# Top-32 attention and a Sinkhorn mixture of experts on one core: the weight tile becomes the work buffer of top-32

## The chip, the core and the metric

The kernel runs on one core of one Trainium2 chip. The metric is the device time of one execution in microseconds. The engines named below are PE (TensorE, matmuls), DVE (VectorE), ACT (ScalarE), POOL (GpSimd) and SP (SyncE, which issues the DMAs here). Each engine takes its own instructions strictly in the order of the program and waits at semaphores for the others.

## What is computed

Two parts follow each other. The first is attention over 4 batches, 8 heads, 576 rows and head size 64, in which each row keeps only its 32 largest scores. The second is a mixture of 8 experts whose gate is balanced by 8 rounds of Sinkhorn normalisation over all 2304 rows.

```
scores = scale * np.matmul(q, k.transpose(0, 1, 3, 2))
kth = np.partition(scores, -top_k, axis=-1)[..., -top_k:-top_k + 1]
scores = np.where(scores >= kth, scores, -1000000000.0)
attn = np.exp(scores - max); attn = attn / (sum + 1e-09)
x = attn @ v
logits = x @ w_gate; P = np.exp(logits - logits.max())
for _ in range(8):
    P /= P.sum(1, keepdims=True) + 1e-09
    P /= P.sum(0, keepdims=True) + 1e-09
    P *= N / E
for e in range(E):
    out += P[:, e:e + 1] * (np.maximum(x @ w1[e], 0.0) @ w2[e])
```

## The kernel before

**Attention.** The work comes in 7 stages (one batch and one or two blocks of 256 query rows each), 80 top-32 jobs in all. A job is a pair of two units of 128 rows (64 jobs; the other 16 have one unit). For a unit PE forms a 128 x 576 tile of scores in PSUM (tile `sp`, L121 and L122), ACT copies it to a score buffer `s` (L130, 3 buffers). `topk` then runs on DVE: four times it takes the 8 largest (MAX8, L140), and between them three times it strikes those 8 out (MATCH_REPLACE8, L143). The first strike reads `s` and writes a work buffer `w` (2 buffers, one for each unit of a pair); the later ones work in `w`. Then ACT makes the weights from `s` and the threshold, in the tile `Et` that holds both units of a pair (L146, L147; 2 buffers), they are normalised (L150 to L156; the reciprocal L151 is on DVE), and PE transposes them (L239, L299) for the product with `v`.

**Experts.** Each visit of an expert loads weights (`wr`, 3 buffers), and splits them into a high part on ACT (`wh`, L80) and a low part on POOL (`wl`, L86), 6 buffers of each. PE multiplies them (L451, L564). ACT and DVE take the hidden values out of PSUM (L519, L520). Visits need only the x of their blocks, so they fill PE while attention goes on. Visits 20 to 23 handle one block of 256 rows alone.

**After attention.** `sinkhorn` runs 8 rounds on DVE; each has one tiny matmul against a tile of ones (L424). Then the attention pools are closed. The last part of the kernel computes the remaining row blocks by a Strassen-like scheme (`hidden_pair`, L675, then L734). Its right factors are built once by `right_factors`: sums `tf` on POOL (L627), high parts on ACT (`B11h`, `T1h`, ..., L80) and low parts on POOL (`B11l`, `T1l`, ..., L86). They live in a pool `x2` that is opened on the same side of the memory as the closed attention pool `ap_`. The left factors are sums on POOL (L661) and a split as above.

**What sets the order.** A scheduler orders the instructions of each engine by priority and by its own estimate of times. Attention has a higher priority than the visits. The tile of ones is allocated in the pool `const`, outside the attention pools:

```
    ones = const.tile([128, 128], F32, name="ones")
    nc.vector.memset(ones, 1.0)

    def sinkhorn():
```

Below, "the work of PE" between two places is the count of its matmuls there.

Of the kernel before, what the change touches and what calls it, by code (L numbers as in the profile page):

```python
# [7 lines left out]
F32 = mybir.dt.float32  # L8
# [4 lines left out]
NB, NH, S, D = 4, 8, 576, 64  # L13
# [28 lines left out]

PARKED = 4
ALONE, LATER = range(0, 4), range(4, 8)
WR, WB, XR, NS, RAW, YB = 3, 6, 3, 3, 3, 4


@with_exitstack
def kernel(
# [11 lines left out]
    nc = tc.nc  # L61
# [3 lines left out]
    const = ctx.enter_context(tc.tile_pool(name="const", bufs=1))  # L65
# [10 lines left out]
    ap_ = actx.enter_context(tc.tile_pool(name="ap", bufs=2, side="right"))  # L76
# [38 lines left out]
    def scores(groups):  # L115
        sp = pss.tile([128, 2, 512], F32, name="sp")
        for dst, terms in groups:
            o = sp[:, dst[0], dst[1]:dst[2]]
            n = len(terms)
            for i, (qc, (kh, kl), cs) in enumerate(terms):  # L120
                nc.tensor.matmul(o, qc, kh[:, cs], start=(i == 0), stop=False)  # L121
                nc.tensor.matmul(o, qc, kl[:, cs], start=False, stop=(i == n - 1))  # L122
        return sp

    def copy_scores(sp):
        s = ap_.tile([128, S], F32, name="s", bufs=NS)
        if sp.shape[-1] == S:
            nc.scalar.activation(s, sp, AF.Copy, scale=0.125)
        else:
            nc.scalar.activation(s.rearrange("p (a b) -> p a b", a=2), sp, AF.Copy, scale=0.125)  # L130
        return s

    def topk(units):
        n = len(units)
        ws = [ap_.tile([128, S], F32, name="w", bufs=2) for _ in units]
        m8 = ap_.tile([128, 2, 4, 8], F32, name="m8", bufs=3)
        eb = ap_.tile([128, 2], F32, name="eb", bufs=3)
        for r in range(4):
            for u in range(n):
                nc.vector.max(m8[:, u, r, :], ws[u] if r else units[u][0])  # L140
            if r < 3:
                for u in range(n):
                    nc.vector.match_replace(ws[u], m8[:, u, r, :], ws[u] if r else units[u][0], LOWEST)  # L143
        nc.gpsimd.tensor_tensor(eb[:, 0:n], m8[:, 0:n, 3, 7], m8[:, 0:n, 0, 0], op=OP.subtract)
        for u, (s, Em, rsum) in enumerate(units):
            nc.scalar.activation(Em, s, AF.Prelu, bias=m8[:, u, 3, 7:8], scale=-1.0, alpha=KEPT)  # L146
            nc.scalar.activation(Em, Em, AF.Exp, bias=eb[:, u:u + 1], scale=-1.0 / KEPT, accum_out=rsum)  # L147

    def normalise(Et, st, n, on_pool=False):
        nc.gpsimd.tensor_scalar(st[:, 0, 0:n], st[:, 0, 0:n], 1e-9, 1.0, op0=OP.add, op1=OP.mult)  # L150
        nc.vector.reciprocal(st[:, 1, 0:n], st[:, 0, 0:n])  # L151
        for i in range(n):
            if on_pool:
                nc.gpsimd.tensor_scalar(Et[:, i, :], Et[:, i, :], st[:, 1, i:i + 1], 1.0, op0=OP.mult, op1=OP.mult)
            else:
                nc.scalar.activation(Et[:, i, :], Et[:, i, :], AF.Copy, scale=st[:, 1, i:i + 1])  # L156
# [62 lines left out]

    def weight_tiles(qs, ks, put, on_pool=False):  # L220
        for t in range(2):
            Et = ap_.tile([128, 2, S], F32, name="Et", bufs=2)
            st = ap_.tile([128, 2, 2], F32, name="st", bufs=3)
            units = []
            for i in range(2):
                o = i * 256 + t * 128
                qc = qs[:, o:o + 128]
                sp = scores([((a, 0, 288), [(qc, ks[i], slice(a * 288, a * 288 + 288))]) for a in range(2)])
                units.append((copy_scores(sp[:, :, 0:288]), Et[:, i, :], st[:, 0, i:i + 1]))
            topk(units)  # L230
            normalise(Et, st, 2, on_pool)
            cs = slice(t * 128, (t + 1) * 128)
            Ef = Et.rearrange("p a b -> p (a b)")
            for g in range(3):
                ps = pst.tile([128, 4, 128], F32, name="pt")
                for r in range(3):
                    j = g * 3 + r
                    o = j * 128 if j < 4 else (j * 128 + 128 if j < 8 else 512)
                    nc.tensor.transpose(ps[:, r, :], Ef[:, o:o + 128], idt)  # L239
                put(slice(g * 3, g * 3 + 3), cs, ps[:, 0:3, :])  # L240
# [43 lines left out]


    def rest_weights(qm, ks, put):
        Et = ap_.tile([128, 2, S], F32, name="Et", bufs=2)
        st = ap_.tile([128, 2, 2], F32, name="st", bufs=3)
        qa, qb = qm[:, 0:128], qm[:, 128:256]
        sp = scores([  # L290
            ((0, 0, 256), [(qa, ks[0], slice(0, 256)), (qb, ks[1], slice(64, 320))]),
            ((0, 256, 512), [(qa, ks[0], slice(256, 512)), (qb, ks[1], slice(320, 576))]),
            ((1, 0, 64), [(qa, ks[0], slice(512, 576)), (qb, ks[1], slice(0, 64))]),
        ])
        topk([(copy_scores(sp.rearrange("p a b -> p (a b)")[:, 0:S]), Et[:, 0, :], st[:, 0, 0:1])])
        normalise(Et, st, 1)
        ps = pst.tile([128, 4, 128], F32, name="pt")
        for j in range(4):
            nc.tensor.transpose(ps[:, j, :], Et[:, 0, j * 128:(j + 1) * 128], idt)  # L299
        for i in range(2):  # L300
            put(slice(0, 128), slice(4 * i, 4 * i + 4), ps[:, :, i * 64:(i + 1) * 64])
        ps = pst.tile([128, 4, 128], F32, name="pt")
        nc.tensor.transpose(ps[0:64, 0, :], Et[:, 0, 512:576], idt)
        nc.tensor.transpose(ps[:, 1, :], Et[:, 0, 448:576], idt)
        for i, r in enumerate((va, vb)):
            put(r, 8, ps[r, i, r])
# [87 lines left out]
                hi_act(seat.xh[:, kk, cs], x[:, kk, :])  # L394
                lo_dve(seat.xl[:, kk, cs], x[:, kk, :], seat.xh[:, kk, cs])

    ones = const.tile([128, 128], F32, name="ones")
    nc.vector.memset(ones, 1.0)

    def sinkhorn():  # L400
        lgf = lg.rearrange("p t e -> p (t e)")
        mx = const.tile([128, 1], F32, name="mx")
        nc.vector.reduce_max(mx, lgf, axis=mybir.AxisListType.X)
        tp = pst.tile([128, 512], F32, name="pt")
        nc.tensor.transpose(tp[:, 0:128], mx.to_broadcast([128, 128]), idt)
        nmx = const.tile([128, 1], F32, name="nmx")
        nc.vector.reduce_max(nmx, tp[:, 0:128], axis=mybir.AxisListType.X)
        nc.vector.tensor_scalar(nmx, nmx, -1.0, None, op0=OP.mult)

        bank = pss.tile([128, 2, 512], F32, name="sp")  # L410
        Q = bank[:, 0, 0:NT * E].rearrange("p (t e) -> p t e", t=NT)
        rp, cp = bank[:, 0, 256:256 + NT], bank[:, 0, 320:320 + E]
        nc.scalar.activation(bank[:, 0, 0:NT * E], lgf, AF.Exp, bias=nmx)
        rs = const.tile([128, NT], F32, name="rs")
        cs = const.tile([128, E], F32, name="cs")
        cr = const.tile([128, E], F32, name="cr")
        for i in range(8):
            nc.vector.reduce_sum(rp, Q, axis=mybir.AxisListType.X)
            nc.vector.tensor_scalar(rp, rp, 1e-9, None, op0=OP.add)
            nc.vector.reciprocal(rs, rp)  # L420
            nc.vector.tensor_tensor(Q, Q, rs[:, :, None].to_broadcast([128, NT, E]), op=OP.mult)
            nc.vector.reduce_sum(cs, Q.rearrange("p t e -> p e t"), axis=mybir.AxisListType.X)
            ct = pst.tile([128, 512], F32, name="pt")
            nc.tensor.matmul(ct[:, 0:E], ones, cs, start=True, stop=True)  # L424
            nc.vector.tensor_scalar(cp, ct[:, 0:E], 1e-9, float(E) / N, op0=OP.add, op1=OP.mult)
            nc.vector.reciprocal(cr, cp)
            nc.vector.tensor_tensor(P if i == 7 else Q, Q, cr[:, None, :].to_broadcast([128, NT, E]), op=OP.mult)
# [412 lines left out]
```

## Time and profile before

| | us |
|---|---|
| median of 3 runs | 1922.92 (1922.9 to 1923.92) |
| the profiled execution, its own time | 1925.95 |
| its span, first to last instruction | 1924.2 |
| PE busy | 1878.1 (98%) |
| DVE busy | 1301.4 (68%) |
| ACT busy | 1108.7 (58%) |
| POOL busy | 1030.8 (54%) |

A busy PE is not PE at its peak, since matmuls overlap in the records; so time is counted here by the distance from one matmul to the next and by the stretches in which PE stands idle. A row of the timeline has the start in us, the busy time of the group in us, the engine, the line, the instruction and its tiles, and in brackets the idle time before it and what ended it.

### The profile page before, as it was taken

What the parts mean: (1) busy time and instruction counts of PE and PEld (TensorE: products, weight loads), DVE (VectorE), ACT (ScalarE), POOL (GpSimd) and SP (SyncE); (2) the same over time, 40 slices, a digit from 0 to 9 for tenths busy, and PEclk for the clock granted to TensorE, in tenths of its full rate; (3) what the DMA queues carried; (4) which work ended last, traced back from release to release, by engine and by line L of the source; (5) the groups of instructions that cost most, each with busy time, mean ns of one, the idle gap of its engine ahead of it and who ended that gap; (6) DMA issues with size and microseconds to landing.
All of it is one profiled execution on the core that took longest, in us unless ns stands there. A gap on an engine that the chain in (4) does not pass through costs nothing.

```text
span 1924.2 us, 27054 instructions
## 1 busy us (share of the span) xinstructions
PE 1878.1 (98%) x9649; PEld 1577.5 (82%) x9649; DVE 1301.4 (68%) x2501; ACT 1108.7 (58%) x1929; POOL 1030.8 (54%) x858
## 2 busy tenths in 40 slices
PE   4999999999999999999999999999999999999998
PEld 3677798988888888888888888888888888888886
DVE  8989999999898996389999432135555555543333
ACT  5878787877777877477786545443333333333331
POOL 3367756565355545455453398855455445455440
PEclk9999999999999999999999999999999999999999
DMA  3686554443233334334432325533333333311101
GB/s 123 232 275 198 181 167 143 148 162 117 94 120 125 125 112 133 119 124 136 136 100 71 114 94 191 176 126 104 110 111 111 118 99 99 95 59 60 61 33 44
DMA packets 96071, 237.91 MB, mean 124 GB/s; under 512 B 10816, under 2 KB 15040, under 8 KB 95936
## 3 DMA queue, kind: packets, MB, share of 16 engines
q1 hardware_dynamic: 95936, 236.19, 38.3%
q8 instruction: 76, 1.25, 0.3%
q14 instruction: 59, 0.48, 0.1%
HBM read 201.54 MB, written 34.60 MB: 123 GB/s over the span
## 4 chain that ended last, share of the span: by engine, by line
PE 85%; POOL 4%; DMA 3%; ACT 3%; issue 2%; DVE 2%; SPq 0%; ACTq 0%; POOLq 0%; DVEq 0%
PE p L564 18%; PE p L451 18%; PE p L734 18%; PE p L675 9%; PE pc L675 5%; PE pt L239 3%; DMA wr<-in_w_dram 2%; PE pb L675 2%; POOL wl L86 2%; PE sp L121 2%; PE sp L122 2%; PE pt L277 2%; PE pt L276 2%; PE pt L253 1%; DVE m L140 1%
## 5 line engine op out<-in xcount | busy, mean ns | idle before, releaser
L86 POOL TENSOR_TENSOR wl<-wr,wh 128x1024 fp32r<-128x1024 f32 x280 | 675.7, 2423 | 474.5 <-ACT wh L80 458.6
L80 ACT ACTIVATE wh<-wr 128x1024 fp32r<-128x1024 f32 x280 | 296.0, 1060 | 313.7 <-PE p L675 193.7
L140 DVE MAX8 m<-w 128x8 f32<-128x576 f32 x432 | 318.4, 750 | 3.5
L451 PE MATMUL p<-xh,wh 128*128 128x256 f32 (+1 forms) x800 | 272.8, 341 | 2.7 <-DVE hl L520 2.1
L451 PE MATMUL p<-xh,wl 128*128 128x256 f32 (+1 forms) x800 | 270.9, 339 | 0.0
L451 PE MATMUL p<-xl,wh 128*128 128x256 f32 (+1 forms) x800 | 270.8, 338 | 0.0
L564 PE MATMUL p<-wh,hh 128*128 128x512 f32 x640 | 252.4, 397 | 5.9 <-ACT hh L519 5.9
L564 PE MATMUL p<-wl,hh 128*128 128x512 f32 x640 | 252.7, 396 | 0.0
L564 PE MATMUL p<-wh,hl 128*128 128x512 f32 x640 | 246.0, 396 | 0.0
L143 DVE MATCH_REPLACE8 w<-m,w 128x576 f32<-128x576 f32 x288 | 213.7, 743 | 0.1
L581 DVE SCALAR_TENSOR_TENSOR acc<-p,P,acc 128x512 f32<-128x512 f32 x120 | 89.5, 750 | 166.7 <-PE p L734 166.7
L734 PE MATMUL p<-wh,h2h 128*128 128x512 f32 x512 | 199.8, 391 | 1.3 <-ACT h2h L698 0.7
L734 PE MATMUL p<-wl,h2h 128*128 128x512 f32 x512 | 199.9, 390 | 0.0
L734 PE MATMUL p<-wh,h2l 128*128 128x512 f32 x512 | 196.7, 390 | 0.0
L520 DVE SCALAR_TENSOR_TENSOR hl<-p,hh 128x512 fp32r<-128x512 f32 x160 | 108.9, 683 | 107.7 <-ACT hh L519 106.6
L451 PEld LDWEIGHTS p<-xh,wh 128*128 128x128 f32 x800 | 152.8, 191 | 19.9 <-DVE hl L520 2.3
L451 PEld LDWEIGHTS p<-xl,wh 128*128 128x128 f32 x800 | 152.7, 191 | 15.4
L451 PEld LDWEIGHTS p<-xh,wl 128*128 128x128 f32 x800 | 152.5, 191 | 14.1
L564 PEld LDWEIGHTS p<-wh,hh 128*128 128x128 f32 x640 | 120.6, 189 | 28.2 <-ACT hh L519 6.8
L564 PEld LDWEIGHTS p<-wl,hh 128*128 128x128 f32 x640 | 120.8, 189 | 22.2
L564 PEld LDWEIGHTS p<-wh,hl 128*128 128x128 f32 x640 | 120.6, 189 | 22.0
L140 DVE MAX8 m<-s 128x8 f32<-128x576 f32 x144 | 108.2, 752 | 44.0 <-ACT s L130 25.6
(185 smaller groups left out, 3889.2 us busy)
## 6 DMA issues: line engine op xcount, KB each, us to landing
wr<-in_w_dram SPq DMA_DIRECT2D x240, 512.0 KB, 3.5
y<-y SPq DMA_DIRECT2D x160, 256.0 KB, 2.7
raw<-in_k_dram SPq DMA_DIRECT2D x56, 288.0 KB, 3.1
raw<-in_q_dram SPq DMA_DIRECT2D x32, 256.0 KB, 3.1
p<-y SPq DMA_DIRECT2D x32, 256.0 KB, 3.6
wr<-in_w_dram SPq DMA_DIRECT2D x32, 256.0 KB, 3.8
y<-p SPq DMA_DIRECT2D x32, 256.0 KB, 4.1
raw<-in_v_dram SPq DMA_DIRECT2D x20, 288.0 KB, 3.1
```

The lines of the kernel that those rows point to most:

```text
L80: nc.scalar.activation(dst, src, AF.Copy)
L86: nc.gpsimd.tensor_tensor(dst, src, hi.bitcast(F32), op=OP.subtract)
L121: nc.tensor.matmul(o, qc, kh[:, cs], start=(i == 0), stop=False)
L140: nc.vector.max(m8[:, u, r, :], ws[u] if r else units[u][0])
L143: nc.vector.match_replace(ws[u], m8[:, u, r, :], ws[u] if r else units[u][0], LOWEST)
L239: nc.tensor.transpose(ps[:, r, :], Ef[:, o:o + 128], idt)
L451: nc.tensor.matmul(ps[:, fo, :], a[:, kk, fs], x[:, k0 + kk, cs], start=(i == 0), stop=(i == 3 * nk - 1))
L520: nc.vector.scalar_tensor_tensor(seat.hl[:, ft, cs], src, 0.0, seat.hh[:, ft, cs].bitcast(F32), op0=OP.max, op1=OP.subtract)
L564: nc.tensor.matmul(ps, a[:, ft, ts], m[:, ft % 2, :], start=(i == 0), stop=(i == 3 * NFT - 1))
L581: return nc.vector.scalar_tensor_tensor(ACC[t], y, g, ACC[t], op0=OP.mult, op1=OP.add)
L675: nc.tensor.matmul(ps, w[:, kk, :], x[:, kk, :], start=(fresh and i == 0), stop=(i == 5), skip_group_check=True)
L734: nc.tensor.matmul(ps, a[:, ft, ts], m[:, ft, :], start=(i == 0), stop=(i == 11))
```

## The change

The work buffer `w` goes: `topk` strikes the largest values out in the weight tile `Et` itself, which ACT overwrites later. `Et` gets a third buffer and the scores a fourth. To make room, `m8` has 2 buffers in place of 3, and the tile of ones becomes one of the `raw` buffers of the attention pool, filled when `sinkhorn` starts. In the new kernel the lines behind L397 have numbers that are one lower (L424 is L423, L564 is L563, L627 is L626, L661 is L660, L675 is L674).

```
-WR, WB, XR, NS, RAW, YB = 3, 6, 3, 3, 3, 4
+WR, WB, XR, NS, RAW, YB = 3, 6, 3, 4, 3, 4
...
     def topk(units):
         n = len(units)
-        ws = [ap_.tile([128, S], F32, name="w", bufs=2) for _ in units]
-        m8 = ap_.tile([128, 2, 4, 8], F32, name="m8", bufs=3)
+        ws = [Em for _, Em, _ in units]
+        m8 = ap_.tile([128, 2, 4, 8], F32, name="m8", bufs=2)
...
-            Et = ap_.tile([128, 2, S], F32, name="Et", bufs=2)
+            Et = ap_.tile([128, 2, S], F32, name="Et", bufs=3)
...
-    ones = const.tile([128, 128], F32, name="ones")
-    nc.vector.memset(ones, 1.0)
-
     def sinkhorn():
+        ones = ap_.tile([128, 128], F32, name="raw", bufs=RAW)
+        nc.vector.memset(ones, 1.0)
```

The scheduler orders the whole program anew. Three places matter below.

POOL of the kernel before, at the start of `right_factors` (`eb` and `st` belong to the last top-32 jobs, `wl` to the visits):

```order
L144 TENSOR_TENSOR eb_9987<-m8_9986 128x1 [waits DVE_49]
L86 TENSOR_TENSOR wl_12234<-wr_12231,wh_12233 128x1024 [waits PE_49,DMAHW0_49,Activation_49,Pool_49]
L150 TENSOR_SCALAR st_9969<-st_9969 128x1 [waits Activation_49]
L86 TENSOR_TENSOR wl_12270<-wr_12267,wh_12269 128x1024 [waits PE_49,DMAHW1_49,Activation_49,Pool_49]
L86 TENSOR_TENSOR wl_12306<-wr_12303,wh_12305 128x1024 [waits DMAHW2_49,PE_49,Activation_49]
L627 TENSOR_TENSOR tf_11330<-xt_8485,xt_11317 128x2x256 [waits DVE_49,Activation_49,Pool_49]
L627 TENSOR_TENSOR tf_11330<-xm_2371,xt_8484 128x2x128
```

The first sum follows the last attention work and waits for that alone. POOL of the new kernel, at the same place:

```order
L86 TENSOR_TENSOR wl_13016<-wr_13013,wh_13015 128x1024 [waits DMAHW4_49,PE_49,Activation_49]
L86 TENSOR_TENSOR wl_13049<-wr_13046,wh_13048 128x1024 [waits DMAHW5_49,PE_49,Activation_49]
L626 TENSOR_TENSOR tf_11186<-xt_8375,xt_11173 128x2x256 [waits PE_49]
L626 TENSOR_TENSOR tf_11186<-xm_2321,xt_8374 128x2x128
L626 TENSOR_TENSOR tf_11186<-xm_5374,xt_8374 128x2x128
L86 TENSOR_TENSOR B11l_11179<-xt_11173,B11h_11178 128x2x256 [waits Activation_49]
```

Many visits' low parts now stand ahead of the first sum, and it waits for PE. Further on in the new kernel, POOL takes the low parts of the next weights between those of the right factors:

```order
L86 TENSOR_TENSOR wl_13082<-wr_13079,wh_13081 128x1024 [waits DMAHW6_49,Activation_49]
L86 TENSOR_TENSOR T1l_11192<-tf_11186,T1h_11191 128x1024 [waits Activation_49]
L86 TENSOR_TENSOR wl_13115<-wr_13112,wh_13114 128x1024 [waits DMAHW7_49,PE_49]
L86 TENSOR_TENSOR wl_13148<-wr_13145,wh_13147 128x1024 [waits DMAHW0_49,PE_49]
L626 TENSOR_TENSOR tf_11226<-xt_11173,tf_11187 128x2x256 [waits Pool_49]
L626 TENSOR_TENSOR tf_11226<-xt_8374,tf_11187 128x2x128 [waits Pool_49]
L86 TENSOR_TENSOR T3l_11215<-tf_11210,T3h_11214 128x1024 [waits Activation_49]
L626 TENSOR_TENSOR tf_11226<-xt_8374,tf_11187 128x2x128 [waits Pool_49]
L86 TENSOR_TENSOR T2l_11207<-tf_11187,T2h_11206 128x1024 [waits Activation_49]
L86 TENSOR_TENSOR wl_13154<-wr_13151,wh_13153 128x1024 [waits DMAHW3_49,PE_49,Activation_49]
L86 TENSOR_TENSOR wl_13160<-wr_13157,wh_13159 128x1024 [waits DMAHW4_49,PE_49,Activation_49]
```

In the kernel before, these were the weights of earlier visits. PE of the new kernel at the last matmul of `sinkhorn`, which reads the tile of ones (`raw_9926`):

```order
L563 MATMUL p2_12955<-wl_12940,hh_97 128x512
L563 MATMUL p2_12955<-wh_12939,hl_98 128x512
L563 MATMUL p2_12955<-wh_12945,hh_97 128x512 [waits Activation_49]
L423 MATMUL pt_10015<-cs_9938,raw_9926 128x8 [waits DVE_49]
L563 MATMUL p2_12955<-wl_12946,hh_97 128x512 [waits Pool_49]
```

That matmul has moved back among the visits: 185 of L564 and 303 of L451 stand between it and the first product of the last part (L675) in the kernel before, 70 and 96 in the new one. 34 and 52 of them stand between it and the first use of `wl_13082`, which is the last row here:

```order
L450 MATMUL p1_13085<-xh_95,wh_13081 128x256 [waits DVE_49]
L450 MATMUL p1_13085<-xl_96,wh_13081 128x256
L450 MATMUL p1_13118<-xh_95,wh_13114 128x256 [waits DVE_49]
L450 MATMUL p1_13118<-xl_96,wh_13114 128x256
L450 MATMUL p1_13085<-xh_95,wl_13082 128x256 [waits Pool_49]
```

On DVE, the 4th top-32 job starts between the strikes of the 3rd; in the kernel before (`w_474` is the work buffer of its first unit, `w_417` that of the job ahead):

```order
L140 MAX m8_418<-w_416 128x8 [waits DVE_49]
L140 MAX m8_418<-w_417 128x8 [waits DVE_49]
L143 MATCH_REPLACE w_474<-m8_476,s_465 128x576 [waits DVE_49]
L143 MATCH_REPLACE w_417<-m8_418,w_417 128x576 [waits DVE_49]
L140 MAX m8_476<-w_474 128x8 [waits DVE_49]
L140 MAX m8_476<-s_472 128x8 [waits Activation_49]
```

In the new kernel (`Et_450` is the weight tile of the 4th job):

```order
L140 MAX m8_466<-s_457 128x8 [waits Activation_49,Pool_49]
L140 MAX m8_410<-Et_394 128x8 [waits DVE_49] x2
L140 MAX m8_466<-s_464 128x8 [waits Activation_49]
L143 MATCH_REPLACE Et_450<-m8_466,s_457 128x576 [waits DVE_49,PE_49]
L143 MATCH_REPLACE Et_394<-m8_410,Et_394 128x576 [waits DVE_49] x2
L151 RECIPROCAL st_176<-st_176 128x2 [waits Pool_49]
```

The first strike of a job now waits for PE, 67 times in the program; in the kernel before none of these strikes did.

## Rows read from the trace of the kernel before

**Rows 1.** The page's first part: busy time, share and instructions.

```profile
PE 1878.1 (98%) x9649; PEld 1577.5 (82%) x9649; DVE 1301.4 (68%) x2501; ACT 1108.7 (58%) x1929; POOL 1030.8 (54%) x858
```

**Rows 2.** Stretches: us, busy time of each engine, granted clock, DMA share, GB/s.

```profile
0.00:60.00 60.00, 33.76 (x130) 23.89 (x131) 53.92 (x114) 36.55 (x69) 20.26 (x29) 1.00 0.44 140
60.00:500.00 440.00, 429.35 (x2595) 368.50 (x2594) 400.74 (x833) 343.87 (x638) 270.17 (x266) 0.99 0.55 177
500.00:1100.00 600.00, 600.00 (x3181) 510.64 (x3180) 499.66 (x1029) 436.63 (x810) 292.51 (x278) 1.00 0.36 116
...
20.00:41.00 21.00, 9.77 (x34) 7.27 (x34) 21.00 (x48) 12.73 (x25) 7.96 (x12) 1.00 0.15 41
...
1200.00:1255.00 55.00, 52.62 (x316) 47.31 (x315) 5.98 (x9) 24.65 (x31) 46.15 (x25) 0.97 0.53 168
...
1214.00:1220.00 6.00, 6.00 (x31) 5.52 (x32) 1.31 (x2) 2.05 (x3) 4.20 (x2) 0.72 0.63 203
```

**Rows 3.** Waits of PE up to 49 us: us in total, times, longest.

```profile
PE sp L121 <- ACT s L130: 18.9, 8, 4.3
```

**Rows 4.** Waits of PE from 49 to 500 us, the largest three.

```profile
PE sp L121 <- ACT s L130: 4.2, 6, 1.6
PE p L564 <- ACT hh L519: 2.8, 2, 1.5
PE p L451 <- DVE hl L520: 2.1, 1, 2.1
```

**Rows 5.** The matmuls of L424: duration ns min/median/max, first and last start.

```profile
L424 PE MATMUL pt<-cs,ones x16: 170/216/256, 1131.2 to 1170.9; 128*128 128x8 f32 x16
```

**Rows 6.** The chain that ended last, 1150 to 1256 us: start, us, what.

```profile
1203.32 1.07 ACT wh L80
...
1204.45 2.41 POOL wl L86
...
1206.88 5.37 DMA wr<-in_w_dram
...
1213.94 1.88 PE p L564 x4
1215.82 3.71 PE p L451 x24
...
1232.81 5.39 PE p L451 x45
...
1245.11 9.77 PE p L564 x43
1254.88 1.16 PE p L675 x5
```

**Rows 7.** POOL in order of time, `right_factors`.

```profile
1107.86 1.30 POOL L627 TENSOR_TENSOR tf<-xt 128x512 f32<-128x512 f32 x1 [4.62 <-DVE xm L282]
...
1122.23 1.44 POOL L86 TENSOR_TENSOR B22l<-xm,B22h 128x256 fp32r<-128x256 f32 x2
1123.63 2.40 POOL L86 TENSOR_TENSOR wl<-wr,wh 128x1024 fp32r<-128x1024 f32 x1
1125.98 1.30 POOL L627 TENSOR_TENSOR tf<-xt,tf 128x512 f32<-128x512 f32 x1
1127.23 2.41 POOL L86 TENSOR_TENSOR T1l<-tf,T1h 128x1024 fp32r<-128x1024 f32 x1
...
1136.65 1.44 POOL L627 TENSOR_TENSOR tf<-xt,tf 128x256 f32<-128x256 f32 x2
```

**Rows 8.** POOL in order of time, sums of the left factors.

```profile
1247.46 3.79 POOL L661 TENSOR_TENSOR wr<-wr 128x256 f32<-128x256 f32 x5
```

**Rows 9.** PE in order of time, its longest late wait.

```profile
1213.94 0.60 PE L564 MATMUL p<-wh,hh 128*128 128x512 f32 x1 [2.38 <-ACT hh L519]
```

**Rows 10.** The chain that ended last, 0 to 200 us: top-32 on DVE.

```profile
12.55 1.98 DVE m L140 x3
14.53 1.46 DVE w L143 x2
```

More of the change, by code (lines that the diff above doesn't have):

```diff
@@ L286, in rest_weights @@
     def rest_weights(qm, ks, put):
-        Et = ap_.tile([128, 2, S], F32, name="Et", bufs=2)
+        Et = ap_.tile([128, 2, S], F32, name="Et", bufs=3)
         st = ap_.tile([128, 2, 2], F32, name="st", bufs=3)
```

## Prediction

> **What bounds the kernel now.** I read the busy times first: PE is busy for 1878.1 of 1924.2 us [rows 1], so the 46 us in which it is not are nearly all that a better order of work can win, and every new idle stretch of PE is a loss in full. The stretches show where they lie [rows 2]: 26 us in the first 60, 10.7 from 60 to 500, none from 500 to 1100, 2.4 from 1200 to 1255. The waits of PE say what ended them. Up to 49 us it is the score copy, 18.9 us [rows 3]; but there DVE is busy for 21.0 of 21 us [rows 2], so top-32 itself is the limit and the score buffers only pass that on. From 49 to 500 us the score copies cost PE 4.2 us and late hidden values 4.9 [rows 4]. In the middle of attention PE never stands still, so freeing DVE or buffers there moves nothing. What is left is the place behind attention, where Sinkhorn, the right factors and the lone visits meet.
>
> **Striking in place.** MATCH_REPLACE8 and MAX8 keep their number and shape; in the steady run three MAX8 take 1.98 us and two strikes 1.46 with the value load [rows 10], about 0.66 to 0.73 us each, in `w` or in half of `Et` alike. I cost this at 0. ACT overwrites `Et` only behind the last MAX8, which it waits for anyway.
>
> **More buffers, in the order of work.** In the new order the first job's last MAX8 is the 22nd top-32 instruction on DVE where it was the 18th, and the second's the 31st where it was the 32nd; the reciprocal of the second, behind which the first attention product waits, stands after 41 of them where it stood after 39. That is 2 x 0.66 = 1.3 us later at the most; I take +1.0. The new wait, 67 first strikes that need the transposes of the job three before, has MAX8s, strikes, and the low parts of hidden and weight values queued behind it on DVE, and PE waits for those low parts. Its price is bounded by the rows on both sides: a gain of the 4.2 us of score waits [rows 4] if the fourth score buffer ends them, a loss of about 3 us where the new order puts transposes some 10 us of PE work earlier (between 200 and 330 us, by my count of matmuls ahead of each job). I take 0, in the middle.
>
> **The tile of ones.** This is the term that decides. The ones now sit in an attention buffer, and the right factors take over that memory. So in the new program the first sum `tf` on POOL and the first high part `B11h` on ACT wait for PE, and the semaphore value is that of the last matmul of Sinkhorn. Before, they needed only the end of attention: the sums started at 1107.86 [rows 7], 23 us before Sinkhorn's first matmul at 1131.2 [rows 5]. Now they start behind Sinkhorn's end, in the middle of the lone visits, where PE has 70 of L564 and 96 of L451 left before the first product (185 and 303 before), and where POOL has little to spare: it is busy 46.15 of 55 us from 1200 to 1255 [rows 2].
>
> The sum, with time 0 at the end of Sinkhorn's last matmul. PE needs 0.120 us for a matmul of L451 (45 in 5.39), 0.227 for L564 (43 in 9.77) and 0.232 for L675 (5 in 1.16) [rows 6]. POOL needs 2.41 us for a full low part, of a weight or a factor [rows 6, 7], 1.30 and 0.72 for the two sizes of `tf` [rows 7], 0.76 for a sum of L661 (5 in 3.79) [rows 8].
>
> - Ahead of the first sum POOL has `wl_13049`. Its buffers come free 5 matmuls of L564 (1.1 us) before time 0; ACT then needs 1.07 and POOL 2.41 [rows 6], so it ends at 2.4. The bounds are 0.2 and 2.4; I take 2.4, since the buffer count leaves no other way.
> - The 17 sums and low parts up to `B22l` took from 1107.86 to 1123.63 = 15.8 us [rows 7], to 18.2; then `wl_13082`, at 20.6. PE comes to it after 34 of L564 and 52 of L451 = 7.7 + 6.2 = 13.9. PE is late by 6.7.
> - `T1l`, two `wl`, three `tf`, `T3l`, `T2l` and `wl_13154`: 6 x 2.41 + 1.30 + 2 x 0.72 = 17.2, so 37.8. PE after 46 and 96: 21.9. Late by 15.9.
> - `wl_13160`, `wl_13166`, `T4l`, two sums, `wl_13243`, five sums, `wl_13247`: 5 x 2.41 + 7 x 0.76 = 17.4, so 55.2. PE after 80, 96 and 20 of L675: 18.2 + 11.5 + 4.6 = 34.3. Late by **20.9**.
> - The next three low parts come some 19 behind PE's own work, so nothing is added.
>
> The DMAs of these weights need 5.37 us at the most [rows 6] and are issued when the low part three before is done, 7.2 us of POOL ahead or more, and ACT's nine high parts run beside POOL's first sums; POOL hides both. The reads of spilled rows behind them on SP's queue are not needed yet.
>
> What falls away: before, 185 of L564 and 303 of L451, 42.0 + 36.4 = 78.4 us of work, lay between Sinkhorn's last matmul at 1170.9 [rows 5] and the first product at 1254.88 [rows 6], 84.0 us. 5.6 us were lost there: waits like the 2.38 us one [rows 9], and the granted clock of 0.72 in the 6 us behind it [rows 2], that is, a part of them at 1.2 GHz, when 24 matmuls of L451 took 3.71 us where 45 take 5.39, and four of L564 took 1.88 [rows 6], together 1.8 us too much. In the new order two thirds of that work stand before Sinkhorn's end with nothing of the right factors in POOL's way; I take the 5.6 as gone. The same low clock will follow the new waits, but there POOL is the limit and hides it, except after the last one: 0 to 1.8, I take 0.9.
>
> Sum: 1.0 + 20.9 - 5.6 + 0.9 = **+17.2 us**. The profiled execution took 1925.95, so a profile of the new kernel should show about 1943; the median of the runs shown is 1922.92, 3.0 lower. I predict 1922.9 + 17.2 = 1940.
>
> **The rivals.**
> *The order of attention turns against PE* (1951). The 67 new waits tie DVE to PE's transposes; where DVE comes there first, low parts that PE needs stand behind the wait. Its place is 50 to 350 us, where DVE is busy 400.74 of 440 us [rows 2] and PE has little in hand; its price is the idle time of PE there once more, 10.7. It decides if a job's first strike comes up before the transposes of the job three earlier are done. For it: by the work counted ahead of each, the two are within about 2 us of each other in the first ten jobs. Against it: such a wait ends as PE moves on, and PE has visits to fill it.
>
> *The late factors are covered* (1921). If PE's 34 us of work were enough, only the 5.6 us would fall away, against the 1.0 of the start and waits of some 3 us. For it: six converted weights can lie ready. Against it: the order on POOL puts 15.8 us of sums ahead of the very next one.
>
> *The buffers win* (1917). If all score waits, 18.9 + 4.2 = 23.1 us [rows 3, 4], went, the sum would be 17.2 - 23.1, so 5.9 faster. It decides where the gain at the start passes 17.2 us, so nearly all of the first 49 us must go. The Trainium skill (Perfetto Trace Analysis, Optimization Strategy) holds that the same gap repeating on the engine that should be saturated can mean that there is not enough memory for the next tile; by that rule the fourth score buffer fills the gaps. The trace disagrees for the start, since DVE has no idle time while PE has these gaps [rows 2], and leaves only 4.2 us of them to the rule.
>
> That the change does not do what it says is out: the program shows the strikes in `Et`.
>
> **How the numbers follow.** Forecast 0.68, order of attention 0.17, covered 0.08, buffers 0.07. A difference under 0.2% (3.8 us) is about what a measurement of this kernel cannot tell from none. The forecast's own bounds are 0.2 for 2.4 in the first step, -4.2 and +4.3 in attention, 0 and 1.8 for the clock: 18.7 - 5.6 - 4.2 = 8.9 to 20.9 - 5.6 + 1.8 + 4.3 = 21.4 us. The range goes from there down by 2 for the sums of POOL and up to the first rival: 1930 to 1951. Slower 0.85, within 0.2% 0.08, faster 0.07.
>
> **What would show it.** Right: PE full up to Sinkhorn's last matmul; at most 1 us between that (or the low part ahead) and the first `tf`; then waits of PE for `wl_13082`, `wl_13115`, `wl_13154`, `wl_13243` and `wl_13247` of some 7, 2, 7, 2 and 2 us, in all 18 to 21; idle time at the start within 3 us of before. Wrong: `tf` running before Sinkhorn's end, PE waits below 8 us between Sinkhorn and the first products, or an idle time from 49 to 500 us that differs from before by more than 6.

## The result, and the profile after

The changed kernel took 1948.0 us (median of five runs, 1941.44 to 1949.14), the kernel before 1922.9: a ratio of 1.0125, with a 95% interval of 1.0108 to 1.0142. The profiled execution took 1948.0 (before 1925.95). All line numbers below are those of the changed kernel, and "behind Sinkhorn" means behind the end of its last matmul (L423).

The page's first part, as [rows 1], and the stretches, as [rows 2]:

```profile
PE 1887.8 (97%) x9649; PEld 1588.0 (82%) x9649; DVE 1288.6 (66%) x2501; ACT 1109.9 (57%) x1929; POOL 1031.3 (53%) x858
```

```profile
0.00:60.00 60.00, 35.03 (x139) 25.11 (x140) 53.54 (x112) 36.51 (x71) 21.27 (x30) 1.00 0.47 144
60.00:500.00 440.00, 426.78 (x2560) 367.34 (x2559) 389.76 (x810) 336.78 (x622) 267.33 (x261) 0.98 0.54 177
...
1100.00:1200.00 100.00, 100.00 (x578) 89.56 (x577) 46.80 (x114) 57.86 (x97) 55.69 (x39) 0.95 0.40 129
1200.00:1300.00 100.00, 85.93 (x453) 73.61 (x453) 22.40 (x56) 45.97 (x64) 93.07 (x64) 0.93 0.41 132
...
1227.00:1282.00 55.00, 40.93 (x203) 34.44 (x202) 5.31 (x10) 22.84 (x35) 54.65 (x43) 0.88 0.31 102
...
1245.00:1270.00 25.00, 15.91 (x71) 13.81 (x72) 1.38 (x2) 7.23 (x8) 25.00 (x14) 0.73 0.26 84
```

PE's idle time at the start (25.0 us) and from 60 to 500 us (13.2) is near that of before (26.2 and 10.7). The largest loss stands in 1227 to 1282: PE (the first busy time) is busy for 40.93 of 55 us and POOL (the fifth) for 54.65. In the middle of it the granted clock is 0.73, which is 13.5 of 25 us at 1.2 GHz in place of 2.4. The waits of PE from 1200 to 1300 us name the same engine:

```profile
PE p L563 <- POOL wl L86: 6.3, 1, 6.3
PE p L450 <- POOL wl L86: 5.4, 1, 5.4
PE pc L674 <- POOL wl L86: 0.9, 1, 0.9
```

Sinkhorn's matmuls and the first product (first and last start at the end of the numbers), and POOL in order of time:

```profile
L423 PE MATMUL pt<-cs,raw x16: 170/214/256, 1183.4 to 1227.1; 128*128 128x8 f32 x16
...
L674 PE MATMUL p<-B11h,wh x64: 387/395/407, 1272.2 to 1889.2; 128*128 128x512 f32 x64
```

```profile
1227.19 2.42 POOL L86 TENSOR_TENSOR wl<-wr,wh 128x1024 fp32r<-128x1024 f32 x1 [1.95 <-ACT wh L80]
1229.56 1.31 POOL L626 TENSOR_TENSOR tf<-xt 128x512 f32<-128x512 f32 x1
...
1245.36 2.39 POOL L86 TENSOR_TENSOR wl<-wr,wh 128x1024 fp32r<-128x1024 f32 x1
...
1261.92 7.09 POOL L86 TENSOR_TENSOR wl<-wr,wh 128x1024 fp32r<-128x1024 f32 x3
...
1278.78 2.39 POOL L86 TENSOR_TENSOR wl<-wr,wh 128x1024 fp32r<-128x1024 f32 x1
```

POOL works without a gap from the first sum on, and three of the low parts of weights that stand among or behind those of the factors end PE's three waits for POOL (they are done at 1247.75, 1264.4 and 1281.2). In [rows 7] the same sums ran from 1107.86 on, ahead of Sinkhorn.

The waits of DVE up to 500 us hold two kinds that the kernel before did not have: strikes that wait for PE's transposes (first row), and first MAX8s of a job that wait for ACT's first pass over the weights (L146) or POOL's `eb`, which read an `m8` buffer two jobs back:

```profile
DVE Et L143 <- PE pt L239: 13.9, 10, 4.4
...
DVE m L140 <- ACT Et L146: 6.0, 3, 2.5
...
DVE m L140 <- POOL eb L144: 1.6, 1, 1.6
```

### The profile page after: what moved, and what is told of

Read it like the earlier page. It is cut to its first block, busy times and chain, and to the rows that moved or that the text cites. A ratio compares the mean times of both kernels' runs of the same rounds, so it can differ in the third digit from the quotient of the medians.

```text
span 1946.1 us, 27147 instructions
## 1 busy us (share of the span) xinstructions
PE 1887.8 (97%) x9649; PEld 1588.0 (82%) x9649; DVE 1288.6 (66%) x2501; ACT 1109.9 (57%) x1929; POOL 1031.3 (53%) x858
## 4 chain that ended last, share of the span: by engine, by line
PE 91%; DVE 3%; POOL 3%; DMA 1%; ACT 1%; issue 1%; SPq 0%; ACTq 0%; POOLq 0%; DVEq 0%
PE p L563 21%; PE p L450 20%; PE p L733 18%; PE p L674 9%; PE pc L674 5%; PE pt L239 3%; PE pb L674 2%; PE sp L121 2%; PE sp L122 2%; PE pt L276 2%; PE pt L253 2%; PE pt L277 2%; PE p L499 1%; POOL wl L86 1%; DVE m L140 1%; DVE Et L143 1%
## 5 line engine op out<-in xcount | busy, mean ns | idle before, releaser
L140 DVE MAX8 m<-Et 128x8 f32<-128x576 f32 x432 | 313.0, 747 | 1.1
L563 PE MATMUL p<-wl,hh 128*128 128x512 f32 x640 | 251.6, 396 | 6.3 <-POOL wl L86 6.3
L563 PE MATMUL p<-wh,hh 128*128 128x512 f32 x640 | 252.6, 398 | 1.6 <-ACT hh L518 1.5
L563 PE MATMUL p<-wh,hl 128*128 128x512 f32 x640 | 245.6, 395 | 0.0
L143 DVE MATCH_REPLACE8 Et<-m,Et 128x576 f32<-128x576 f32 x288 | 212.9, 742 | 0.1
L563 PEld LDWEIGHTS p<-wl,hh 128*128 128x128 f32 x640 | 121.1, 189 | 28.9 <-POOL wl L86 6.7
L563 PEld LDWEIGHTS p<-wh,hh 128*128 128x128 f32 x640 | 120.9, 190 | 24.4 <-ACT hh L518 2.8
L563 PEld LDWEIGHTS p<-wh,hl 128*128 128x128 f32 x640 | 120.7, 189 | 22.2
```

The lines of the kernel that those rows point to most:

```text
L563: nc.tensor.matmul(ps, a[:, ft, ts], m[:, ft % 2, :], start=(i == 0), stop=(i == 3 * NFT - 1))
```

## Theories and experiments

**Theory A** is that of the prediction: the memory of the ones makes the right factors late, and POOL's sequence behind Sinkhorn sets PE's waits. **Theory B**: the loss sits in attention, in its new order and the 67 strikes that wait for PE. Theories with other letters are named in the expectation of the run that they belong to. A table of what was run; each ratio is to the kernel before on the same chip, with its 95% interval, and between runs the ratios are compared, since not all ran on one chip.

| ones in | strikes in | Et, s, m8 buffers | other | median us | ratio |
|---|---|---|---|---|---|
| raw | w | 2, 3, 3 | | 1941.1 | 1.0102 (1.0081 to 1.0123) |
| y | w | 2, 3, 3 | | 1921.8 | 1.0001 (0.9989 to 1.0013) |
| raw | Et | 3, 4, 2 | the changed kernel again | 1950.1 | 1.0140 (1.0122 to 1.0158) |
| y | Et | 3, 4, 2 | | 1932.4 | 1.0059 (1.0039 to 1.0079) |
| y | Et | 3, 3, 2 | | 1929.7 | 1.0045 (1.0027 to 1.0064) |
| y | Et | 3, 3, 3 | | 1927.5 | 1.0023 (1.0011 to 1.0035) |
| y | w | 2, 3, 2 | | 1928.3 | 1.0025 (1.0016 to 1.0035) |
| y | Et | 2, 4, 2 | | 1950.0 | 1.0141 (1.0123 to 1.0158) |
| raw | Et | 3, 4, 2 | factors' low parts on DVE | 1935.7 | 1.0062 (1.0046 to 1.0077) |
| const | w | 2, 3, 3 | factors' low parts on DVE | 1924.0 | 1.0008 (0.9996 to 1.0021) |
| y | Et | 3, 3, 3 | factors' low parts on DVE | 1922.7 | 0.9996 (0.9988 to 1.0005) |

**The ones alone, put into the kernel before.**

```
-    ones = const.tile([128, 128], F32, name="ones")
-    nc.vector.memset(ones, 1.0)
     def sinkhorn():
+        ones = ap_.tile([128, 128], F32, name="raw", bufs=RAW)
+        nc.vector.memset(ones, 1.0)
```

> The kernel before with one edit: the tile of ones is a raw buffer of the attention pool; strikes, Et, m8 and the three score buffers stay as before, and so does the order of attention. Theory A (the late right factors are the loss): POOL's first tf waits for Sinkhorn's last matmul, and 153 matmuls of L563 and 288 of L450 (69.2 us of PE's work, against 27.4 in the changed kernel) stand between that and the first product. POOL's sequence, reckoned with the durations of the prediction, is then late by 3.8, 2.1, 5.8 and 1.3 us at four low parts, 13.0 in all; less the 5.6 lost there before and plus 0.9 for the clock: +8.3 us, 1931 (1927 to 1936). Theory B (the new order of attention and the 67 strikes that wait for PE are the loss): none of that is in this kernel, so 1923 (1920 to 1926).

Measured: +1.02%, 19 us, and so theory A, but 11 us more than it said, and above its range. Waits of PE from 1175 to 1260, the last matmul of Sinkhorn, POOL's first sum, and the first product:

```profile
PE p L563 <- POOL wl L86: 11.7, 3, 7.1
PE p L563 <- ACT hh L518: 1.7, 2, 1.3
PE p L450 <- ACT wh L80: 1.0, 1, 1.0
```

```profile
L423 PE MATMUL pt<-cs,raw x16: 170/214/256, 1129.7 to 1179.1; 128*128 128x8 f32 x16
...
1183.31 1.30 POOL L626 TENSOR_TENSOR tf<-xt 128x512 f32<-128x512 f32 x1
...
L674 PE MATMUL p<-B11h,wh x64: 387/395/398, 1268.4 to 1881.0; 128*128 128x512 f32 x64
```

The idle time, 14.4 us, is near the 13.0 expected. But from the end of Sinkhorn's last matmul, 1179.3, to 1268.4 pass 89.1 us for 69.2 of work: 19.9 are lost. Two low parts of weights, not one, stood ahead of the first sum, which began 4.1 us behind Sinkhorn in place of 2.4, and PE's work between the waits ran partly at 1.2 GHz. When the last large wait ended, at 1218.1, 38.8 us had passed for 22.9 of work by the count of matmuls, 15.9 late where the expectation has 11.7. The other 4 were lost behind it, where POOL was the limit no more: 1.3 in a wait for a hidden value (second row), and some 2 because nothing hid the low clock there (0.69 from 1218 to 1224). The 5.6 that were to fall away were not all there to win either (below).

**The ones elsewhere, in the kernel before and in the changed one.** In both the tile becomes

```
+        ones = op_.tile([128, 512], F32, name="y", bufs=YB)[:, 0:128]
```

> The kernel before with one edit: the tile of ones is a y buffer of the output pool, filled when sinkhorn starts. Every engine has the order of before. Theory A: where the ones are costs nothing as long as the right factors do not take over that memory: 1923 (1920 to 1926). Rival: that the ones are made and freed inside sinkhorn costs by itself (a y buffer held for some 40 us makes the outputs wait, of which four buffers exist): 1927 or more, with waits of PE or DVE for y between 1130 and 1175.

> The changed kernel with one edit: the tile of ones is a y buffer of the output pool, outside the memory that the right factors take over; in-place strikes, three Et and four score buffers stay, and attention has the same order of instructions as in the changed kernel. Theory A: POOL's first tf comes ahead of Sinkhorn's end again and the 19 us between 1050 and the first product go; what is left is the 3 to 5 us by which attention itself runs later: 1927 (1923 to 1931). Theory B: the loss sits in attention and stays: 1942 or more.

Measured: in the kernel before no difference (1.0001, 0.9989 to 1.0013), so being made and freed inside `sinkhorn` costs nothing that shows. In the changed kernel 0.0059 are left of 0.0125 and 0.0140: of some 25 us, 14 go and 11 stay. From Sinkhorn's end to the first product pass 42.5 us for 41.9 of work:

```profile
L423 PE MATMUL pt<-cs,y x16: 170/256/277, 1184.1 to 1215.5; 128*128 128x8 f32 x16
...
L674 PE MATMUL p<-B11h,wh x64: 387/395/398, 1258.1 to 1872.4; 128*128 128x512 f32 x64
```

Theory A holds for this half. The 11 us that stay are more than its 3 to 5 (1932.4 lies just above its range), so attention costs more than the prediction had.

**The changed kernel again.** No edit; a second profile.

> The changed kernel once more, with a second profile. Theory D: the 10.24 us of half clock that its profile showed from 1166.7, right behind the 32 gate-logit matmuls of L368, belong to this order of PE's work and come again at the same place (6 us or more there); then 3 to 5 us of the loss are theirs. Rival: they were chance; then 3.41 us or nothing there and a time some 3 us lower. Either way the waits of PE for low parts between 1240 and 1285 come again with 12 to 14 us. Time 1945 (1941 to 1950).

Measured: the same waits (first two rows), and the same fall of the clock from 1166 on (third row; 0.57 over 12 us is 10.3 us at 1.2 GHz), while PE was busy without a gap (12.00 of 12). The other two rows are the same place in the kernel before and in a run that comes further down, the changed kernel with the factors' low parts on DVE:

```profile
PE p L563 <- POOL wl L86: 6.3, 1, 6.3
PE p L450 <- POOL wl L86: 5.3, 1, 5.3
```

```profile
1166.00:1178.00 12.00, 12.00 (x62) 11.90 (x62) 2.27 (x6) 2.73 (x7) 3.62 (x2) 0.57 0.26 88
```

```profile
1115.00:1119.00 4.00, 4.00 (x13) 3.14 (x12) 0.00 (x0) 1.88 (x3) 4.00 (x6) 0.57 0.00 0
```

```profile
1164.00:1176.00 12.00, 12.00 (x64) 10.85 (x64) 3.63 (x11) 4.62 (x7) 4.82 (x3) 0.86 0.36 121
```

The kernel before has 3.4 us of it (0.57 over 4 us). So this run speaks for theory D. But the run with the low parts on DVE has the same matmuls in the same order on PE, from the first to the last, and there the fall lasted 3.4 us as well (0.86 over 12 us). The order of PE's work alone does not decide it, and theory D is not shown.

**What attention loses, taken apart.** First the score buffers (`NS` 4 to 3, ones in y), then `m8` in the kernel before and in that one:

```
-WR, WB, XR, NS, RAW, YB = 3, 6, 3, 4, 3, 4
+WR, WB, XR, NS, RAW, YB = 3, 6, 3, 3, 3, 4
```

> The changed kernel with the ones in a y buffer and three score buffers in place of four; in-place strikes and three Et stay. Against the run with four score buffers it gives the worth of the fourth, and against the kernel before that of in-place strikes with a third Et. Theory A (both small): PE idle in the first 60 us 25 to 27, from 60 to 500 us 10 to 14, time 1925 (1920 to 1930). Theory B (the strikes' 67 waits for PE cost): the third Et is all they have here too, so 1935 or more, with over 16 us idle from 60 to 500. Theory C (the fourth score buffer gains at the start and hides a loss of the strikes): 3 us or more slower than the run with four.

```
-        m8 = ap_.tile([128, 2, 4, 8], F32, name="m8", bufs=3)
+        m8 = ap_.tile([128, 2, 4, 8], F32, name="m8", bufs=2)
```

> The kernel before with the ones in a y buffer (which by itself cost nothing) and m8 with two buffers in place of three: the one part of the change that the prediction gave no price. 22 first MAX8 of a job now wait for POOL's eb two jobs before, where none did. Strikes go to w as before. Theory M (the two m8 buffers are part of what attention loses): new idle time of DVE before MAX8 behind POOL eb or ACT Et, 3 us or more up to 500 us, and 1925 or more (to 1929). Rival S (only the strikes' waits for PE count): 1922 (1920 to 1924).

```
-        m8 = ap_.tile([128, 2, 4, 8], F32, name="m8", bufs=2)
+        m8 = ap_.tile([128, 2, 4, 8], F32, name="m8", bufs=3)
```

> In-place strikes, three Et, three score buffers, the ones in a y buffer, and m8 with three buffers: the run with three score buffers (1929.7) with the one difference that m8 keeps its third buffer. 56 strikes wait for PE in both. Theory M: 2 to 4 us faster than that run, 1926 (1924 to 1928). Rival S: no different, 1930 (1928 to 1932).

Measured: the fourth score buffer gains nothing (1932.4 with it, 1929.7 without), against theory C, and the time without it is at the upper end of theory A's; PE's idle time from 60 to 500 us, 15.2 in its profile, lies between the 10 to 14 of theory A and the 16 of theory B. Two `m8` in place of three cost the kernel before 0.25%, about 5 us. Putting the third back gains some 2 to 4 us in the other, where the intervals overlap. Theory M's time is right. Its mechanism is not shown: in the kernel before with two `m8`, DVE's new idle time behind `eb` and Prelu up to 500 us is 1.8 us, less than the 3 expected:

```profile
DVE m L140 <- ACT Et L146: 1.0, 1, 1.0
DVE m L140 <- POOL eb L144: 0.8, 2, 0.5
```

What changes as well is the order that the scheduler makes with them (on PE it differs from about the 410th matmul on); that this order is the cost is argued and not shown. The stretch from 60 to 500 us, of the kernel before with the ones in y, then with two `m8`, then with strikes in Et and three of Et, s and m8, and last with four scores and two `m8`:

```profile
60.00:500.00 440.00, 431.26 (x2612) 371.89 (x2610) 403.43 (x838) 345.86 (x643) 270.18 (x268) 0.99 0.54 178
```

```profile
60.00:500.00 440.00, 428.27 (x2595) 369.15 (x2594) 403.62 (x844) 345.75 (x643) 268.75 (x270) 0.99 0.55 178
```

```profile
60.00:500.00 440.00, 427.62 (x2592) 368.84 (x2591) 402.04 (x837) 344.69 (x635) 271.14 (x266) 0.99 0.54 175
```

```profile
60.00:500.00 440.00, 424.97 (x2569) 366.09 (x2569) 392.55 (x814) 337.65 (x622) 268.94 (x263) 0.99 0.55 176
```

PE's idle time there is 8.7, 11.7, 12.4 and 15.0 us: small waits of many kinds.

**Two weight tiles.** The changed kernel with the ones in y and

```
-            Et = ap_.tile([128, 2, S], F32, name="Et", bufs=3)
+            Et = ap_.tile([128, 2, S], F32, name="Et", bufs=2)
```

> The changed kernel with the ones in a y buffer and two Et in place of three, four score buffers: the first strike of a job now waits for the transposes of the job two before, not three (77 such waits). It doubles the suspected cost of striking in place. Theory S (in-place strikes tie DVE to PE, and only the third Et keeps that short): DVE idle behind PE's transposes up to 500 us 60 us or more, where the run with three had 13; attention ends much later, visits run out before Sinkhorn, and the time is 1960 to 2020. Rival (PE reaches the transposes soon enough and fills with visits, so the wait is free): within 5 us of the run with three, 1932 (1927 to 1937).

Measured: some 16 us slower than with three (1.0141 against 1.0059). So striking in place does tie DVE to PE, but theory S named too high a price: the time stays 10 us under its 1960, and the strikes' waits up to 500 us are 29.8 us, not 60:

```profile
DVE Et L143 <- PE pt L239: 29.8, 16, 5.4
```

The end of top-32 shows how far attention falls behind. The last MAX8 of the kernel before, of the one with strikes in Et and three of Et, s and m8, of the changed kernel, and of this one:

```profile
L140 DVE MAX8 m<-w x432: 701/750/765, 9.2 to 1074.6; 128x8 f32<-128x576 f32 x144
```

```profile
L140 DVE MAX8 m<-Et x432: 695/749/764, 9.2 to 1112.4; 128x8 f32<-128x576 f32 x144
```

```profile
L140 DVE MAX8 m<-Et x432: 700/747/764, 9.3 to 1130.7; 128x8 f32<-128x576 f32 x144
```

```profile
L140 DVE MAX8 m<-Et x432: 730/749/765, 9.6 to 1216.8; 128x8 f32<-128x576 f32 x144
```

Top-32 ends 38, 56 and 142 us later. PE fills nearly all of that with visits, and pays with the stock of visits that is left to cover Sinkhorn and the right factors: between Sinkhorn's last matmul and the first product stand visits of 78.3, 47.5, 27.4 and 0 us of PE's work.

**The main cost by itself: POOL's sequence.** The low parts of the right factors go to DVE, in the changed kernel, in the kernel before, and in the best one so far:

```
-                lo_pool(l[:, :, cs], src, h[:, :, cs])
+                lo_dve(l[:, :, cs], src, h[:, :, cs])
```

> The changed kernel (ones in a raw buffer, four scores, three Et, two m8) with one edit: the low parts of the right factors (B11l to T4l) are formed on DVE in place of POOL. They still cannot start ahead of Sinkhorn's last matmul. Theory P (POOL's sequence behind Sinkhorn is what PE waits for): 8.0 us of B11l, B21l and B22l and 4 x 2.4 of T1l to T4l, 17.6 in all, leave POOL's sequence ahead of wl_13247, whose lateness was 20.9; PE's waits for POOL's low parts between Sinkhorn's end and the first product fall from 12 us to 3 or less, and the time to 1949 - 16 = 1933 (1929 to 1937). Rival W (the weight buffers, their transfers or ACT's high parts are the limit there): the waits stay under other names and the time is 1944 or more.

> The kernel before with the same edit: low parts of the right factors on DVE. There they run ahead of Sinkhorn, with POOL only 23 us ahead of need. Theory P: nothing waits for them, so 1922 (1919 to 1925). Rival: DVE's part beside Sinkhorn's steps delays these: 1926 or more.

> The run with in-place strikes, three Et, three scores, three m8 and the ones in a y buffer (1927.5), with the low parts of the right factors on DVE. There PE still lost some 5 us between 1100 and 1180: 1.8 us in one wait for a low part of POOL, 1.6 in one for Sinkhorn, and the rest at half the granted clock (6.83 us from 1149.2 and 6.83 from 1169.7). Theory P: the wait for POOL goes and with it the second stretch of half clock: 1924 (1920 to 1927). Rival: no different, 1928 (1926 to 1930).

Measured: theory P in all three. With the ones still in the raw buffer, 12 to 15 of some 25 us go (0.0062 are left of 0.0125 and 0.0140); PE's waits for POOL's low parts from 1200 to 1300 us fall from 12.6 to 0.7, and the one large wait left is for a hidden value's low part that now queues on DVE behind those of the factors:

```profile
PE p L450 <- DVE hl L519: 4.1, 1, 4.1
...
PE pc L674 <- POOL wl L86: 0.7, 1, 0.7
```

Its profile shows what of the gain stands behind Sinkhorn:

```profile
L423 PE MATMUL pt<-cs,raw x16: 170/214/256, 1175.5 to 1219.2; 128*128 128x8 f32 x16
...
L674 PE MATMUL p<-B11h,wh x64: 387/395/408, 1253.9 to 1870.6; 128*128 128x512 f32 x64
```

From the last L423 to the first product pass 34.7 us where the changed kernel needs 45.1, so 10.4 are won there. Another 7.9 us, by which Sinkhorn itself ends earlier, are not a gain of the edit: PE's order is the same in both, and this profile is of the fastest of the six runs, 6 us under their median.

In the kernel before the move is worth nothing. In the third it gains 5 us and ends even with the kernel before (0.9996). No version beat the kernel before. A fourth score buffer together with three `m8` was not tried, as the memory does not hold it.

## Why the prediction came out as it did

Forecast +17.2 us, measured +24 and, in the later run, +27; the sign, the place and the mechanism of the main term are those of the forecast, two terms are mis-sized. The measured 1948 lies above the sum's own bounds (8.9 to 21.4 us, which is up to 1944). It is inside the stated range because that range was drawn up to the first rival's 1951, which adds 10.7 us of idle time in attention to the sum. Attention did cost about as much, but for the most part by other ways than that rival's (below), so that the range held is in part luck.

- **The late right factors, 20.9: right.** The first sum started 2.4 us behind Sinkhorn (1229.56 against 1227.2), as worked out. `wl_13082` was done at 20.5 (20.6 worked out), `wl_13154` at 37.2 (37.8), `wl_13247` at 54.0 (55.2). PE resumed there at 1281.2 with 34.3 us of work done in 54.0: 19.7 lost. Of the five named waits, 18 to 21 us in sum, three came, of 5.4, 6.3 and 0.9, and the idle time was 14.1 in all (55 - 40.93), because PE's work between them ran partly at 1.2 GHz. The prediction had said that POOL hides this, and so it did.
- **The clock behind the last wait, 0.9:** nothing; all of the low clock lies in 1245 to 1270, ahead of the last wait.
- **The old loss that falls away, 5.6: too large.** It was read from one profile. The same matmuls, in the kernel before with the ones in y, have the last L423 at 1169.4 (done 0.2 later) and the first product at 1250.9 in the rows below: 81.3 us for 78.3 of work, so 3.0.

```profile
L423 PE MATMUL pt<-cs,y x16: 170/215/256, 1129.6 to 1169.4; 128*128 128x8 f32 x16
...
L674 PE MATMUL p<-B11h,wh x64: 392/395/398, 1250.9 to 1863.5; 128*128 128x512 f32 x64
```

- **Start and attention, +1.0 within -4.2 and +4.3: mis-sized, and this is the step that failed.** With the factors out of the way 11 us are left (ratio 1.0059). The two first profiles say 7.5: Sinkhorn's last matmul stands at 1227.1 with 29.7 us of the visits' work still to come, in the kernel before at 1170.9 with 78.4. Three things bear on them. `m8` with two buffers had no term at all; it costs the kernel before some 5 us by itself. Strikes in place with a third `Et`, priced at the middle of a gain and a loss, cost 4 (1.0023); these went when the low parts moved to DVE (0.9996). From 1100 to 1200 us PE then stood idle for 1.2 us in place of 3.4, at a granted clock of 0.97 in place of 0.93; so they are paid at the right factors, which a later end of attention leaves with less cover. The last is the granted clock, which the sum did not count ahead of Sinkhorn: 10.2 us at 1.2 GHz behind the gate logits where the kernel before has 3.4, and 17.0 up to 500 us where it has 6.8 (0.98 and 0.99 in the stretches). That is 8.5 us of PE's work more as an upper bound, in part chance (the run with the low parts on DVE has 3.4 behind the gate logits), and it overlaps with the other two. The prediction's sign, idle time from 49 to 500 us, rose by only 2.2, as it does not see the clock. The strikes themselves do cost nothing: MATCH_REPLACE8 takes 742 ns at the median in `Et` and 743 in `w`.
- **The rivals.** *The order of attention* is nearer to the measured time than the forecast, and it named a wait that is there, the strikes' 13.9 us for PE. But its price was not paid as it said: idle time from 60 to 500 us rose from 10.7 to 13.2 us in the profile after (8.7 to 15.0 between the two with the ones in y), not by 10.7. *Covered* is out. *The buffers win* is out: the score waits up to 49 us went from 18.9 [rows 3] to 13.7, but PE now waits 4.8 us for weight tiles there, and the idle time up to 60 us is 25.0 against 26.2 [rows 2]. The rule of the Trainium skill (Perfetto Trace Analysis, Optimization Strategy) that a repeating gap can mean too little memory does not hold here: a fourth score buffer gained nothing (1.0059 with it, 1.0045 without).

PE's waits up to 49 us:

```profile
PE sp L121 <- ACT s L130: 13.7, 7, 5.5
...
PE pt L239 <- POOL Et L154: 4.8, 2, 3.9
```

Both errors made the forecast too low, by 2.6 and by 6.5 to 10 us; the first two terms were 2.1 too high. Together that is about the gap of 7 to 10 between 17.2 and 24 to 27. Which small waits of attention come from which buffer is not settled, because each buffer count makes the scheduler order the program anew.

## What to carry to other kernels

A buffer that is moved into a shared pool brings that pool's next tenant with it: look up who takes over the memory, and what its last reader is. Work done in place saves memory and pays with a wait, here of DVE for PE three jobs back; even when PE fills the wait with other work, it spends the filler that a later stage lives on. Give each buffer count that a change lowers a term of its own, small tiles too.

## What the runs showed of the hardware

DVE and POOL held each other up when both subtracted from two operands at once. With the low parts on DVE in the changed kernel, three instructions of the same kind and size on DVE:

```profile
1231.45 3.40 DVE L89 TENSOR_TENSOR T1l<-tf,T1h 128x1024 fp32r<-128x1024 f32 x1
1234.77 1.74 DVE L89 TENSOR_TENSOR T3l<-tf,T3h 128x1024 fp32r<-128x1024 f32 x1
...
1237.63 2.19 DVE L89 TENSOR_TENSOR T2l<-tf,T2h 128x1024 fp32r<-128x1024 f32 x1
```

and POOL beside them:

```profile
1231.20 2.57 POOL L86 TENSOR_TENSOR wl<-wr,wh 128x1024 fp32r<-128x1024 f32 x1
1233.73 1.70 POOL L626 TENSOR_TENSOR tf<-xm,tf 128x256 f32<-128x256 f32 x1
1235.39 3.35 POOL L86 TENSOR_TENSOR wl<-wr,wh 128x1024 fp32r<-128x1024 f32 x1
1238.70 2.26 POOL L626 TENSOR_TENSOR tf<-xt,tf 128x512 f32<-128x512 f32 x1
```

Each of the three ended 1.08 us behind the end of the POOL instruction that was under way when it began: `T1l` at 1234.85 behind 1233.77, `T3l` at 1236.51 behind 1235.43, `T2l` at 1239.82 behind 1238.74. POOL's own sum took 1.70 where [rows 7] have 0.72, and the `wl` behind it 3.35 where they have 2.40. So part of what was taken off POOL came back as waiting inside the instructions. That may be why the gain was 12 to 15 us and not the 17.6 of POOL's time that was moved; it was not tested. The Trainium skill (SBUF — State Buffer, SBUF: two separate sides) says that DVE with two SBUF inputs and GpSimd lock a shared pair of ports for a whole instruction, the one that starts first blocking the other; these rows agree with it.

The other thing not expected was the clock: at the 32 gate-logit matmuls of 128x8 (L368) it fell to 1.2 GHz while PE's records show no gap. It stayed there for 10.2 us in both profiles of the changed kernel, and for 3.4 us in the kernel before and in the changed kernel with the low parts on DVE. The last has the same matmuls in the same order on PE as the first two, so neither their order nor their shapes alone set how long the clock stays low. What does is open.
